# Two blocks of an ELU layer finish their exponential on ScalarE; the ELU becomes a minimum of two terms

## The chip, the cores and the metric

The kernel runs on one core of a Trainium2 chip. The metric is the time of one execution on the device, in microseconds (us); lower is better. The five engines of the core are called PE (TensorE, matrix products), DVE (VectorE), ACT (ScalarE), POOL (GpSimd) and SP (SyncE, which issues DMAs here).

## What is computed

Attention with a bucket mask, then a feed-forward layer with ELU, then a second one with a scaled squared ReLU. The matrices are float32; the result is float32, 1536 tokens by 512.

```python
# attention: q, k, v are (2, 8, 768, 64); a key counts only in the query's bucket (6 sign bits of a projection)
scores = where(q_bucket == k_bucket, scale * q @ k.T, -1e9)
attn   = softmax(scores);  x = concat_heads(attn @ v)          # (1536, 512)
# first layer: w_in (512, 2048), w_out (2048, 512)
h = x @ w_in
g = where(h > 0, h, exp(min(h, 0)) - 1)                        # ELU
x2 = g @ w_out
# second layer, other weights of the same shapes
out = (s * max(x2 @ w_in2, 0) ** 2 + b) @ w_out2
```

## The kernel before

Every float32 product is made of three float16 products (high by high, high by low, low by high), so each operand is split into a high and a low half. `products` (L503) issues these matmuls.

**Attention** goes by units: 2 batches x 6 row chunks x 8 heads = 96 units `u`. Unit `u` makes scores on PE (`u_s`, L336), clamps them with a running minimum on DVE (`u_soft`, L346, `p<-s`), adds a constant to that minimum (L347, `mx`), takes the exponential on ACT (L348), rounds to float16 on ACT (`u_split`, L367, `ph`), subtracts on POOL for the low half (L370), turns both halves by a DMA that SP issues (L372, `pt<-ph`), and multiplies by v on PE (`u_av`, L390, `xacc`). After eight heads `u_norm` (L401) writes a chunk of x. For the first 16 units PE does the turning instead.

**Weights** come as 64-bit words and are put together on DVE. `w_stream` (L165) handles one piece of 512 columns per step: a DMA into `wraw` (L162), three integer operations on DVE (L182, L183 into a PSUM tile `wx`, L185 into `wa`), ACT rounds the high half (L176: `wih`, `woh`), DVE makes the low half (L189: `wil`, `wol`). `w_in` and `w_out` are 16 pieces each. Before the attention of the second batch begins (from unit 38 on, `att_step`, L733), all pieces that are left are run one behind the other. Their buffers are then given to the loads of k, q and v of the second batch (L233).

**The first layer** (`moe1`, L549) goes in six blocks of 256 tokens. `up(i)` makes 8 PSUM tiles `h` of 128x512 from `wi`; each is handed to `act1` (L509), whose steps run beside the products of the next tiles: `exp` on ACT (L514, `e` from PSUM), `elu` on DVE (L517 and L519), `hi` on ACT (L522, `gh`), `lo` on POOL (L525, `gl`). `down(i)` multiplies `gh` and `gl` by `wo` into `x2p`. Units of attention are put between the products by a credit of estimated time (L742 to L749). The last part, `moe2`, is the second layer.

The order in which each engine takes its instructions is fixed at build time: the framework's scheduler works it out with a model of the engines, from the order of the code and the priorities. So another instruction in `act1` can change places all along the middle of the program. Each engine then takes its instructions in that order and waits where an operand is not there. SP issues its DMAs in order too.

In `act1`, with `SG` = 512 the factor by which h is scaled: `e` = exp(h); then `e` = min(SG e, SG) (L517); then `g` = max(e - SG, SG h) (L519).

Of the kernel before, what the change touches and what calls it, by code (L numbers as in the profile page):

```python
# [11 lines left out]
ACTF = mybir.ActivationFunctionType  # L12
ALU = mybir.AluOpType
# [32 lines left out]
W2OUT = 4  # L46
D2 = 200
SPLIT = lambda u: 'act'
WEV = lambda k: k % 3
W2EV = lambda k: k % 4 == 0  # L50
STEP_COST = 2.5
# [7 lines left out]
def model_kernel(tc, q, k, v, proj, w_in, w_out, w_in2, w_out2, s2, b2, sel, pop, eye, out):  # L59
    nc = tc.nc  # L60
# [18 lines left out]
    SG = SX * SW  # L79
# [4 lines left out]
    with ExitStack() as base:  # L84
# [267 lines left out]
        def u_split(u, eng):  # L352
            f = pf.pop(u)
            if u < FC * H:
                p = ps_p[0].tile([128, S], F32, tag="s", name="pT")
                for cc in range(C):
                    nc.tensor.transpose(p[:, 128 * cc:128 * cc + 128], f[:, 128 * cc:128 * cc + 128], ident)
                o = ring.take("pt", [128, S], F32, "pt")
                if eng == "act":
                    nc.scalar.activation(out=o, in_=p, func=ACTF.Copy)  # L360
                else:
                    nc.vector.tensor_copy(out=o, in_=p)
                pt[u] = o
                return
            t = ring.take("ph", [128, 2, S], F16, "ph")
            if eng == "act":
                nc.scalar.activation(out=t[:, 0, :], in_=f, func=ACTF.Copy)  # L367
            else:
                nc.vector.tensor_copy(out=t[:, 0, :], in_=f)
            nc.gpsimd.tensor_tensor(out=t[:, 1, :], in0=f, in1=t[:, 0, :], op=ALU.subtract)  # L370
            o = ring.take("pt", [128, 2 * C, 128], F16, "pt")
            nc.sync.dma_start_transpose(out=o, in_=t.rearrange("p x s -> p (x s)"))  # L372
            pt[u] = o
# [76 lines left out]
        def attention():  # L450
# [4 lines left out]
            while nxt["av"] < NU:  # L455
                if nxt["split"]:
                    u_split(nxt["split"].pop(0), SPLIT(nxt["s"]))
                u = nxt["av"]
# [25 lines left out]
        def staged():  # L484
            queue = []

            def add(stages):
                queue.append([0, stages])

            def run(order):  # L490
                for item in queue:
                    for lag, o, fn in item[1]:
                        if lag == item[0] and o == order:
                            fn()

            def tick():
                for item in queue:
                    item[0] += 1
                while queue and all(st[0] < queue[0][0] for st in queue[0][1]):
                    queue.pop(0)  # L500
            return add, run, tick

        def products(p, ws, xs, kks, n_kk):  # L503
            for kk in kks:
                for z, (a, b) in enumerate(((0, 0), (0, 1), (1, 0))):
                    nc.tensor.matmul(p, ws[a](kk), xs[b](kk), start=(kk == 0 and z == 0),  # L506
                                     stop=(kk == n_kk - 1 and z == 2))

        def act1(tmp, tmpg, p, gh, gl):  # L509
            t = {}  # L510

            def exp():
                t["e"] = tmp.tile([128, 512], F32, tag="e", name="e")
                nc.scalar.activation(out=t["e"], in_=p, func=ACTF.Exp, scale=1.0 / SG)  # L514

            def elu():
                nc.vector.tensor_scalar(t["e"], t["e"], SG, SG, op0=ALU.mult, op1=ALU.min)  # L517
                t["g"] = tmpg.tile([128, 512], F32, tag="g", name="g")
                nc.vector.scalar_tensor_tensor(out=t["g"], in0=t["e"], scalar=-SG, in1=p, op0=ALU.add, op1=ALU.max)  # L519

            def hi():
                nc.scalar.activation(out=gh, in_=t["g"], func=ACTF.Copy)  # L522

            def lo():
                nc.gpsimd.tensor_tensor(out=gl, in0=t["g"], in1=gh, op=ALU.subtract)  # L525
            return [(2, 0, hi), (1, 1, exp), (3, 2, lo), (1, 3, elu)]
# [22 lines left out]
        def moe1(wi, wo, gp, next_gp, tmp, tmpg, att_step):  # L549
            add, run, tick = staged()  # L550

            def slot(cost):
                run(0)
                run(1)
                run(2)
                yield cost
                run(3)
                tick()

            starts = [sum(BLOCKS1[:i]) * 128 for i in range(len(BLOCKS1))]  # L560
            g = {}

            def up(i):
                n = 128 * BLOCKS1[i]
                while done_chunks[0] < sum(BLOCKS1[:i + 1]):
                    att_step()
                cost = 12 * (n / 2400 + .003)
                gh, gl = g[i] = [gp[0].tile([128, KF, n], F16, tag=f"g{x}", name=f"g{x}") for x in "hl"]
                w_ = 512 // n
                i2, o2 = divmod(starts[i], 512)  # L570
                for f0 in range(0, KF, w_):
                    p = ring.take("m", [128, 512], F32, "h")
                    for f in range(f0, f0 + w_):
                        xs = [lambda kk, o=o: xx[i2][:, o + kk, o2:o2 + n] for o in (0, KM)]
                        ws = [lambda kk, w=w: w[:, f, kk * 128:kk * 128 + 128] for w in wi]
                        o = p[:, (f - f0) * n:(f - f0) * n + n]
                        products(o, ws, xs, range(KM), KM)
                        if f < f0 + w_ - 1:
                            yield cost
                    add(act1(tmp, tmpg, p, *(z[:, f0:f0 + w_, :].rearrange("p f n -> p (f n)") for z in (gh, gl))))  # L580
                    yield from slot(cost)
                in_done[0] = i + 1

            def down(i):
                n = 128 * BLOCKS1[i]
                cost = 12 * (n / 2400 + .003)
                i2, o2 = divmod(starts[i], 512)
                w_ = 512 // n
                for d0 in range(0, KM, w_):
                    p = ring.take("m", [128, w_, n], F32, "x2p")  # L590
                    for d in range(d0, d0 + w_):
                        xs = [lambda kk, z=z: z[:, kk, :] for z in g[i]]
                        ws = [lambda kk, w=w: w[:, kk, d * 128:d * 128 + 128] for w in wo]
                        for part in range(4):
                            products(p[:, d - d0, :], ws, xs, range(4 * part, 4 * part + 4), KF)
                            if part == 3 and d == d0 + w_ - 1:
                                xh, xl = (xx[i2][:, z * KM + d0:z * KM + d0 + w_, o2:o2 + n] for z in range(2))

                                def hi(p=p, xh=xh):
                                    nc.scalar.activation(out=xh, in_=p, func=ACTF.Copy, scale=SX2 / (SG * SW))  # L600

                                def lo(p=p, xh=xh, xl=xl):
                                    nc.vector.scalar_tensor_tensor(out=xl, in0=p, scalar=SX2 / (SG * SW), in1=xh,  # L603
                                                                   op0=ALU.mult, op1=ALU.subtract)
                                add([(1, 0, hi), (1, 3, lo)])
                            yield from slot(cost)

            for i in range(FIRST):
                yield from up(i)
            for i in range(FIRST):  # L610
                yield from down(i)
            for _ in range(4):
                yield from slot(0)
            next_gp()
            for i in range(FIRST, len(BLOCKS1)):
                yield from up(i)
                yield from down(i)
            for _ in range(4):
                yield from slot(0)
# [63 lines left out]
        if True:  # L683
# [12 lines left out]
            n = 0  # L696
# [11 lines left out]
            tmp = pool(w1st, "tmp", 2)  # L708
            tmpg = pool(w1st, "tmpg", TG)
# [3 lines left out]
            def next_gp():  # L713
                gst0.close()
                gp[0] = pool(gst1, "gp1", 1)
# [17 lines left out]
            def att_step():  # L733
                while live["w1"] and nxt["s"] >= (C - 1) * H - 2:
                    w1_step()
                if next(att, 0) == 0:
                    live["att"] = False
# [4 lines left out]
            for ks, cost in enumerate(moe1(wi, wo, gp, next_gp, tmp, tmpg, att_step)):  # L742
                if WEV(ks):
                    w1_step()
# [81 lines left out]
```

## Time and profile before

| | us |
|---|---|
| median of 3 runs (lowest, highest) | 740.74 (739.79, 742.73) |
| the profiled execution, its own time | 743.25 |
| its span, first to last instruction | 741.1 |
| PE busy in the span | 676.0 |
| DVE busy | 470.6 |
| ACT busy | 375.5 |
| POOL busy | 264.2 |

The profile records each instruction of one execution with its engine and source line. From it come: busy times by stretch of the span, groups of instructions by line, the waits (who sat idle until whom), the timeline, and the chain of work that ended last, followed back from the last instruction. "DMA share" is the mean busy share of the 16 DMA engines; it can pass 1, because packets overlap. "PEclk" is the granted clock of PE as a part of full speed. A wait for several things is put down to the one that came last.

### The profile page before, as it was taken

Reading aid. Unit: us, or ns where it says so; the run is one execution under the profiler, and the core shown is the slowest. Engines: PE = TensorE matmul, PEld = TensorE weight load, DVE = VectorE, ACT = ScalarE, POOL = GpSimd, SP = SyncE. Lnnn points to the kernel's source line nnn. Section 1 sums busy time; section 2 is a strip of 40 time slices with the busy share of each in tenths; the row PEclk is TensorE's granted clock in tenths of the full one; section 3 lists DMA queues with packets and bytes.
Section 4 is the critical chain, followed back from the end, with each engine's and each line's share of the span. In section 5 each row is a group of like instructions: output and inputs, shape, how many; then the busy total and the mean of one; then the engine's idle time right before and its main releaser. Section 6 shows DMA issues by size and latency. Waiting matters only on the chain.

```text
span 741.1 us, 14402 instructions
## 1 busy us (share of the span) xinstructions
PE 676.0 (91%) x5808; PEld 466.2 (63%) x5808; DVE 470.6 (63%) x890; ACT 375.5 (51%) x632; POOL 264.2 (36%) x199
## 2 busy tenths in 40 slices
PE   2689787888897899899999999999999999999998
PEld 0368576766685677788888988864444444444446
DVE  5789998999876557645644684348988989100000
ACT  2897776762777688756755323235555543010000
POOL 0000356660562358945855412214445441000000
PEclk9999989999999999999999999999999999999999
DMA  9954699897699959967758450001322314010000
GB/s 234 267 165 138 158 220 208 184 202 204 95 230 208 180 95 179 155 107 132 122 108 120 124 172 1 1 29 58 115 76 71 110 57 142 1 57 29 29 28 29
DMA packets 206594, 89.67 MB, mean 121 GB/s; under 512 B 171840, under 2 KB 203072, under 8 KB 206528
## 3 DMA queue, kind: packets, MB, share of 16 engines
q1 hardware_dynamic: 205936, 88.63, 54.6%
q8 instruction: 45, 0.74, 0.4%
q10 hardware_dynamic: 592, 0.14, 0.1%
q14 instruction: 21, 0.17, 0.1%
HBM read 43.13 MB, written 3.15 MB: 62 GB/s over the span
## 4 chain that ended last, share of the span: by engine, by line
PE 61%; DVE 15%; DMA 12%; ACT 6%; issue 4%; SPq 1%; POOL 0%; DVEq 0%; ACTq 0%; POOLq 0%
PE h L506 25%; PE y L506 17%; PE x2p L506 11%; DMA pt<-ph 6%; PE s L336 4%; DVE p L346 3%; PE xacc L390 3%; DVE e L517 2%; DMA q<-src 2%; DVE wx L182 1%; DVE wx L183 1%; DVE g L519 1%; ACT p L348 1%; DMA k<-srcl 1%; DMA raw<-in_k 1%
## 5 line engine op out<-in xcount | busy, mean ns | idle before, releaser
L370 POOL TENSOR_TENSOR ph<-p,ph 128x768 f16<-128x768 f32 x80 | 135.5, 1699 | 144.1 <-ACT ph L367 121.1
L506 PE MATMUL h<-x,wih 128*128 128x256 f16 x768 | 134.6, 279 | 0.9 <-DVE g L519 0.9
L348 ACT ACTIVATE p<-p,mx 128x768 f32<-128x768 f32 x96 | 89.2, 929 | 53.3 <-DVE mx L347 51.7
L346 DVE TENSOR_SCALAR_CACHE_REDUCE p<-s 128x768 f32<-128x768 f32 x96 | 90.8, 950 | 38.9 <-PE s L336 37.2
L506 PE MATMUL x2p<-gh,woh 128*128 128x256 f16 x384 | 105.1, 275 | 2.8 <-DVE x L603 1.0
L506 PE MATMUL h<-x,wil 128*128 128x256 f16 x384 | 107.1, 279 | 0.0
L506 PE MATMUL x2p<-gh,wol 128*128 128x256 f16 x384 | 105.4, 275 | 0.7 <-DVE wol L189 0.7
L506 PE MATMUL x2p<-gl,woh 128*128 128x256 f16 x384 | 105.3, 275 | 0.0
L336 PE MATMUL s<-k,q 128*128 128x512 f16 (+1 forms) x384 | 80.0, 334 | 12.9 <-DVE p L346 9.4
L546 POOL TENSOR_TENSOR g2l<-g,g2h 128x512 f16<-128x512 f32 x48 | 56.8, 1188 | 88.2 <-ACT g2h L543 88.2
L506 PE MATMUL h<-x,wi2bh 128*128 128x512 f16 x288 | 85.7, 379 | 0.0
L506 PEld LDWEIGHTS <-wih 128*128 128x128 f16 x768 | 76.5, 100 | 14.4 <-issue 1.8
L506 PEld LDWEIGHTS <-woh 128*128 128x128 f16 x768 | 75.3, 99 | 14.7 <-issue 1.7
L390 PE MATMUL xacc<-vv,pt 128*128 128x64 f16 x1440 | 56.6, 195 | 22.3 <-DMA pt<-ph 22.0
L525 POOL TENSOR_TENSOR gl<-g,gh 128x512 f16<-128x512 f32 x48 | 57.4, 1198 | 52.8 <-ACT gh L522 52.7
L506 PE MATMUL y<-wo2h,g2h 128*128 128x512 f16 (+1 forms) x208 | 75.4, 363 | 0.0
L506 PE MATMUL y<-wo2l,g2h 128*128 128x512 f16 (+1 forms) x208 | 75.4, 363 | 0.0
L506 PE MATMUL y<-wo2h,g2l 128*128 128x512 f16 (+1 forms) x208 | 75.3, 363 | 0.0
L390 PEld LDWEIGHTS <-pt 128*128 128x128 f16 x1440 | 52.1, 99 | 31.8 <-DMA pt<-ph 29.8
L367 ACT ACTIVATE ph<-p 128x768 f16<-128x768 f32 x80 | 66.5, 837 | 5.5 <-DMA pt<-ph 3.7
L506 PEld LDWEIGHTS <-g2h 128*128 128x128 f16 x416 | 40.7, 98 | 42.4
L657 ACT ACTIVATE y<-y 128x512 f32<-128x512 f32 (+1 forms) x13 | 7.3, 564 | 97.8 <-PE y L506 96.8
(101 smaller groups left out, 1109.3 us busy)
## 6 DMA issues: line engine op xcount, KB each, us to landing
wraw<-in_moe_w_in SPq DMA_DIRECT2D x32, 512.0 KB, 3.8
wraw<-in_moe_w_out SPq DMA_DIRECT2D x32, 512.0 KB, 3.7
raw<-in_k SPq DMA_DIRECT2D x8, 384.0 KB, 4.3
raw<-in_q SPq DMA_DIRECT2D x8, 384.0 KB, 4.1
out<-y SPq DMA_DIRECT2D x11, 256.0 KB, 2.0
v<-in_v SPq DMA_DIRECT2D x4, 384.0 KB, 4.7
raw<-in_v SPq DMA_DIRECT2D x4, 384.0 KB, 4.3
pt<-ph SPq DMA_TRANSPOSE x80, 4.0
```

The lines of the kernel that those rows point to most:

```text
L182: nc.vector.tensor_scalar(x, top, 3, 0x3FFFFFFF, op0=ALU.logical_shift_left, op1=ALU.bitwise_and)
L183: nc.vector.scalar_tensor_tensor(out=x, in0=low, scalar=29, in1=x, op0=ALU.logical_shift_right, op1=ALU.bitwise_or)
L336: nc.tensor.matmul(p[:, a0:a1], w[b, hp][:, j, c, :], kf[:, a0:a1], start=(x == 0), stop=(x == 1))
L346: nc.vector.tensor_scalar(f, sps.pop(u), CLAMP, None, op0=ALU.min, op1=ALU.min, accum_out=mx)
L348: nc.scalar.activation(out=f, in_=f, func=ACTF.Exp, scale=-sm / (SQ * SQ), bias=mx, accum_out=sums[b, c][:, h:h + 1])
L367: nc.scalar.activation(out=t[:, 0, :], in_=f, func=ACTF.Copy)
L370: nc.gpsimd.tensor_tensor(out=t[:, 1, :], in0=f, in1=t[:, 0, :], op=ALU.subtract)
L390: nc.tensor.matmul(acc, o[:, C * x + cc, :], vv[:, j, cc, y, :], start=(z == 0 and cc == 0), stop=(z == 2 and cc == C - 1))
L506: nc.tensor.matmul(p, ws[a](kk), xs[b](kk), start=(kk == 0 and z == 0), stop=(kk == n_kk - 1 and z == 2))
L517: nc.vector.tensor_scalar(t["e"], t["e"], SG, SG, op0=ALU.mult, op1=ALU.min)
L525: nc.gpsimd.tensor_tensor(out=gl, in0=t["g"], in1=gh, op=ALU.subtract)
L546: nc.gpsimd.tensor_tensor(out=gl, in0=t["g"], in1=gh, op=ALU.subtract)
```

## The change

The ELU is written as min(max(h, 0), exp(h) - 1), all scaled by `SG`. `SG e - SG` is made in place, in blocks 0 and 1 by a second ACT instruction right behind the exponential (L517 of the changed kernel, a copy with scale and bias), in blocks 2 to 5 by DVE (one `tensor_scalar` as before, with multiply and add in place of multiply and minimum). DVE's last operation then takes the maximum with 0 of the PSUM tile `h` and the minimum with `e`. The new function `LIN` picks the engine by the number of the block.

```diff
+LIN = lambda i: 'act' if i < 2 else 'dve'
...
-        def act1(tmp, tmpg, p, gh, gl):
+        def act1(tmp, tmpg, p, gh, gl, lin):
             t = {}
             def exp():
                 t["e"] = tmp.tile([128, 512], F32, tag="e", name="e")
                 nc.scalar.activation(out=t["e"], in_=p, func=ACTF.Exp, scale=1.0 / SG)
+                if lin == "act":
+                    nc.scalar.activation(out=t["e"], in_=t["e"], func=ACTF.Copy, scale=SG, bias=-SG)
             def elu():
-                nc.vector.tensor_scalar(t["e"], t["e"], SG, SG, op0=ALU.mult, op1=ALU.min)
+                if lin == "dve":
+                    nc.vector.tensor_scalar(t["e"], t["e"], SG, -SG, op0=ALU.mult, op1=ALU.add)
                 t["g"] = tmpg.tile([128, 512], F32, tag="g", name="g")
-                nc.vector.scalar_tensor_tensor(out=t["g"], in0=t["e"], scalar=-SG, in1=p, op0=ALU.add, op1=ALU.max)
+                nc.vector.scalar_tensor_tensor(out=t["g"], in0=p, scalar=0.0, in1=t["e"], op0=ALU.max, op1=ALU.min)
...
-                    add(act1(..., gh, gl))
+                    add(act1(..., gh, gl, LIN(i)))
```

In the order of the changed kernel, 16 instructions `e<-e` have gone from DVE to ACT and 32 are left on DVE. ACT still has one load of its function table, as before. The order of the work around blocks 0 and 1 changes on every engine. Line numbers of the changed kernel are 1 higher up to the exponential, and 5 higher from L519 on.

The first place is DVE's order at the last tiles of block 0, where the pieces of `w_out` are being put together (L182 to L189; `p,mx` and `mx` are the attention). Before:

```order
L346 TENSOR_SCALAR p,mx<-s 128x768
L182 TENSOR_SCALAR wx<-wraw 128x512
L517 TENSOR_SCALAR e<-e 128x512
L347 TENSOR_SCALAR mx<-mx 128x1
L346 TENSOR_SCALAR p,mx<-s 128x768
L189 SCALAR_TENSOR_TENSOR wol<-wa,woh 128x4x128
L183 SCALAR_TENSOR_TENSOR wx<-wraw,wx 128x512
L519 SCALAR_TENSOR_TENSOR g<-e,h 128x512
L517 TENSOR_SCALAR e<-e 128x512
L347 TENSOR_SCALAR mx<-mx 128x1
```

Now, the same tiles:

```order
L347 TENSOR_SCALAR p,mx<-s 128x768
L348 TENSOR_SCALAR mx<-mx 128x1
L524 SCALAR_TENSOR_TENSOR g<-h,e 128x512
L186 SCALAR_TENSOR_TENSOR wa<-wraw,wx 128x512
L347 TENSOR_SCALAR p,mx<-s 128x768
L348 TENSOR_SCALAR mx<-mx 128x1
L524 SCALAR_TENSOR_TENSOR g<-h,e 128x512
L183 TENSOR_SCALAR wx<-wraw 128x512
```

The `e<-e` are gone from DVE, and `g<-h,e` stands between the same kinds of work.

The second place is ACT at the end of the weight stream, where the pieces that are left are run together (`woh`, 128x4x128), followed by the first tiles of block 1. Before:

```order
L348 ACTIVATE p,sum<-p,mx 128x768 x2
L367 ACTIVATE ph<-p 128x768 x2
L176 ACTIVATE woh<-wa 128x4x128
L348 ACTIVATE p,sum<-p,mx 128x768
L367 ACTIVATE ph<-p 128x768
L600 ACTIVATE x_113<-x2p 128x2x256
L176 ACTIVATE woh<-wa 128x4x128 x7
L514 ACTIVATE e<-h 128x512 x2
L348 ACTIVATE p,sum<-p,mx 128x768 x2
L600 ACTIVATE x_113<-x2p 128x2x256
```

Now:

```order
L177 ACTIVATE woh<-wa 128x4x128
L368 ACTIVATE ph<-p 128x768
L349 ACTIVATE p,sum<-p,mx 128x768
L368 ACTIVATE ph<-p 128x768
L177 ACTIVATE woh<-wa 128x4x128 x5
L515 ACTIVATE e<-h 128x512 x2
L349 ACTIVATE p,sum<-p,mx 128x768
L517 ACTIVATE e<-e 128x512
L349 ACTIVATE p,sum<-p,mx 128x768
L517 ACTIVATE e<-e 128x512
L605 ACTIVATE x_113<-x2p 128x2x256
```

Seven pieces stood together at the end of the stream before; five do now, and two have moved up among the units of attention. The new ACT instructions of block 1 stand between two exponentials of the attention.

## Rows read from the trace of the kernel before

**Rows 1.** The page: busy time of each engine, share of the span, instructions.

```profile
PE 676.0 (91%) x5808; PEld 466.2 (63%) x5808; DVE 470.6 (63%) x890; ACT 375.5 (51%) x632; POOL 264.2 (36%) x199
```

**Rows 2.** Busy time of each engine by stretch of the span (us).

```profile
core 0: us, PE busy (x) PEld busy (x) DVE busy (x) ACT busy (x) POOL busy (x), PEclk, DMA share, GB/s
95.00:182.00 87.00, 72.47 (x848) 57.60 (x846) 82.41 (x148) 51.76 (x91) 45.02 (x29) 0.96 0.96 206
182.00:220.00 38.00, 34.81 (x366) 28.74 (x364) 31.69 (x63) 26.29 (x48) 21.67 (x16) 0.96 0.82 148
...
200.00:220.00 20.00, 19.20 (x220) 15.87 (x219) 17.01 (x32) 14.55 (x26) 13.25 (x11) 0.91 1.18 215
...
320.00:340.00 20.00, 20.00 (x251) 17.07 (x248) 9.63 (x21) 10.40 (x17) 11.02 (x7) 1.00 0.69 121
...
440.00:460.00 20.00, 20.00 (x185) 17.94 (x184) 8.56 (x13) 4.65 (x8) 3.47 (x3) 1.00 0.15 45
...
130.00:135.00 5.00, 4.12 (x50) 3.47 (x49) 5.00 (x9) 4.36 (x8) 3.43 (x2) 1.00 0.63 165
...
150.00:155.00 5.00, 3.97 (x47) 3.10 (x45) 5.00 (x8) 1.13 (x2) 3.36 (x3) 1.00 0.85 206
```

**Rows 3.** DVE by line, 95 to 182 us: busy, mean ns, idle before.

```profile
L189 DVE SCALAR_TENSOR_TENSOR wol<-wa,woh 128x512 f16<-128x512 f32 x15 | 13.3, 886 | 0.0
L517 DVE TENSOR_SCALAR e<-e 128x512 f32<-128x512 f32 x8 | 7.6, 945 | 0.1
```

**Rows 4.** The chain that ended last: start, length, what.

```profile
101.72 7.17 DMA pt<-ph
...
131.53 1.76 DVE e L517
...
137.08 1.51 DVE e L517
...
141.32 1.38 DVE e L517
...
205.05 1.82 DVE e L517
...
209.51 0.60 DVE e L517
```

**Rows 5.** Timeline of DVE and of POOL near three `e<-e` and one `wol`.

```profile
101.14 0.43 DVE L517 TENSOR_SCALAR e<-e 128x512 f32<-128x512 f32 x1
...
102.40 1.65 POOL L370 TENSOR_TENSOR ph<-p,ph 128x768 f16<-128x768 f32 x1 [2.55 <-ACT ph L367]
...
137.08 1.51 DVE L517 TENSOR_SCALAR e<-e 128x512 f32<-128x512 f32 x1
...
136.67 1.64 POOL L370 TENSOR_TENSOR ph<-p,ph 128x768 f16<-128x768 f32 x1
...
152.28 1.99 DVE L189 SCALAR_TENSOR_TENSOR wol<-wa,woh 128x512 f16<-128x512 f32 x1
```

**Rows 6.** Tile `wa`, 164 to 183 us: ns shortest/median/longest, first and last start.

```profile
L176 ACT ACTIVATE woh<-wa x7: 619/630/631, 165.1 to 181.8; 128x512 f16<-128x512 f32 x7
L189 DVE SCALAR_TENSOR_TENSOR wol<-wa,woh x7: 681/691/693, 166.4 to 182.4; 128x512 f16<-128x512 f32 x7
```

**Rows 7.** Waits, 145 to 182 us, and SP's own, 95 to 182 us: total, times, longest.

```profile
ACT woh L176 <- DVE wa L185: 13.4, 7, 2.5
...
SPq L233 <- DVE wa L185: 2.7, 1, 2.7
```

**Rows 8.** L517 alone: DVE busy by stretch.

```profile
182.00:220.00 38.00, 5.82 (x8) 0.96 0.82 148
95.00:182.00 87.00, 7.56 (x8) 0.96 0.96 206
```

**Rows 9.** The page: costliest groups, nearest forms to the new instructions.

```profile
L539 DVE SCALAR_TENSOR_TENSOR g<-h,r 128x512 f32<-128x512 f32 x48 | 33.0, 688 | 15.3 <-ACT r L535 14.9
...
L519 DVE SCALAR_TENSOR_TENSOR g<-e,h 128x512 f32<-128x512 f32 x48 | 32.7, 684 | 3.0
L522 ACT ACTIVATE gh<-g 128x512 f16<-128x512 f32 x48 | 29.9, 626 | 38.1 <-DVE g L519 37.8
```

More of the change, by code (lines that the diff above doesn't have):

```diff
@@ L579, in up @@
                             yield cost
-                    add(act1(tmp, tmpg, p, *(z[:, f0:f0 + w_, :].rearrange("p f n -> p (f n)") for z in (gh, gl))))
+                    add(act1(tmp, tmpg, p, *(z[:, f0:f0 + w_, :].rearrange("p f n -> p (f n)") for z in (gh, gl)), LIN(i)))
                     yield from slot(cost)
```

## The prediction

> **What bounds the kernel now.** I read the engines' totals first, then their busy time by stretch, the chain, and last the lines and the timeline of the stretch that the change touches. PE is busy for 676.0 us of 741.1 [rows 1], and from 320 us on it has next to no gap: 20.00 of 20 us in each of the seven windows from 320 to 460 [rows 2]. So nothing that is saved behind 320 us can pay unless it makes PE's own work shorter, and the change does not touch that. Ahead of 320 us PE has gaps, and a gap closed there moves the whole saturated rest forward by as much. Blocks 0 and 1 of the ELU lie in that part: eight `e<-e` between 95 and 182 us, eight between 182 and 220 us [rows 8].
>
> In the first of these stretches PE is busy for 72.47 of 87 us, 14.5 us idle. DVE is busy for 82.41, idle for only 4.6; ACT has 51.76 and POOL 45.02 [rows 2]. DVE sets the pace: it must put the pieces of `w_out` together and clamp the scores of the units up to 38, and only then can the second batch begin. DVE is busy for 5.00 of 5 us in each of the five windows from 130 to 155 us [rows 2], and there the chain runs over DVE, with three `e<-e` on it (1.76, 1.51, 1.38) [rows 4]. At the end of the stretch seven pieces stand in a row, and ACT waits 13.4 us for DVE's `wa` [rows 7]. SP's load of k for the second batch waits 2.7 us for the same `wa` [rows 7]. But DMA is a near second: its share is 0.96 over these 87 us [rows 2], and ahead of 129 us the chain waits for turned tiles, once for 7.17 us [rows 4].
>
> **Part 1, block 0, DVE.** Eight `e<-e` go, 7.56 us [rows 8], mean 945 ns [rows 3]. One of them takes 0.43 us at 101.14, in the 2.55 us in which POOL is idle ahead of 102.40; another takes 1.51 us, begins at 137.08 while a POOL subtraction runs from 136.67 to 138.31, and ends at 138.59, a fast one's length behind it [rows 5]. So an `e<-e` is some 0.42 us of work and otherwise waiting for POOL: 8 x 0.42 = 3.4 us of work, 4.2 us of waiting. The work is saved for certain. The waiting can come back: `wol` waits in the same manner (1.99 us once, mean 886 over 15) [rows 5, 3]. POOL is busy for about half the stretch (45 of 87) [rows 2], so I let half the waiting return at the next such instruction: 2.1 us. Saved: 3.4 + 2.1 = 5.5 us; the ends are 3.4 and 7.6. The order says where it lands: two of the seven pieces move up among the attention, and the `woh` of the seven begin from 165.1 to 181.8 us, (181.8 - 165.1) / 6 = 2.8 us apart [rows 6], so the run ends 5.6 us sooner, if unit 38 comes no later than now. I take 5.5.
>
> Does DMA allow it? Its load in the stretch is 0.96 x 87 = 83.5 us, and in 81.5 us it would be a share of 1.02. A share of 1.18 stands in the window at 200 us [rows 2], so this is possible, but little is left. If it is not, the low end of this part is 0.
>
> **Part 2, block 0, ACT.** Eight copies are added. No such instruction is in the trace; the nearest is L522, SBUF to SBUF, 626 ns [rows 9]. 8 x 0.626 = 5.0 us, which brings ACT from 51.76 to 56.8 of 87. It has 35 us of idle time there, 13.4 of them waiting for DVE's pieces [rows 7], so I cost this at nothing. Behind each copy in ACT's order stand an exponential or a rounding of the attention, and POOL, SP's turning DMA and PE's `xacc` behind those; if the cover were gone, the price is the 5.0. For the single tile, 0.626 on ACT replaces a mean of 0.945 on DVE, so the way from `h` to `g` gets no longer.
>
> **Part 3, block 1.** DVE loses 5.82 us [rows 8], of which two instances lie on the chain, 1.82 + 0.60 = 2.4 us [rows 4]. ACT gains 5.0 again, on 26.29 of 38 us [rows 2]: 31.3, or 82%. Here ACT also makes the k and q halves of the second batch, and its new copies stand between exponentials. I let half of the 5.0 fall on the path: 2.5 against 2.4, so 0. The ends: 2.4 saved, or 5.0 - 2.4 = 2.6 lost.
>
> **Part 4, the rest.** In blocks 2 to 5 `e<-e` keeps its shape with another second operation. `g` takes the PSUM tile first and compares instead of adding: the trace has that form, 688 ns against 684 [rows 9], 48 x 0.004 = 0.2 us, beside a saturated PE: nothing. From about unit 68 on PE's order is as before.
>
> Sum: 5.5 + 0 + 0 + 0 = 5.5 us off the span, 741.1 to 735.6. The profiled execution took 743.25, 2.15 over its span, and 2.5 over the median; I take the 5.5 from the median: 740.7 - 5.5 = **735.2 us**. What is late next is DMA, whose share is 1.18 from 200 us on [rows 2].
>
> **Rivals.**
>
> *The waits only move.* Each POOL subtraction holds up the next DVE instruction of that kind instead, and only 3.4 us are saved: 737.3 us. For it: `wol` already shows such waits, with a mean of 886 ns against 691 in the run of seven [rows 3, 6]. Against: half of the waiting returning is already in the sum, and it would have to be all of it. The Trainium skill, "SBUF — State Buffer", section "Who interferes with whom", says that VectorE's two-port forms and those with two SBUF inputs share a port pair with GpSimd as an exclusive lock, the loser blocked for the whole instruction; the trace agrees (1.51 us beside the 1.64 of POOL). By that rule the lock goes to whoever comes first, so a freed wait may go to `wol`.
>
> *DMA takes over.* With 0.96 the turned tiles and weight loads are already at their limit, the two pieces that move up (their loads too, on SP's queue ahead of turning DMAs) make `xacc` wait longer, and what DVE saves becomes idle time of DVE: nothing to 1.5 us, say 740.0 us. For it: the waits of up to 7.17 us in the chain ahead of 129 us [rows 4]. Against: DVE has no gap from 130 to 155 us while DMA's share is 0.63 and 0.85 in the first and the last of these windows [rows 2].
>
> *ACT takes over, slower.* In 182 to 220 us ACT stands at 82% with the copies, and each one sits ahead of an exponential or of a k or q half. If all eight delay the units, 5.0 us are lost there, and if DMA also eats block 0's gain, the time is 740.7 + 5.0 = 745.7 us. It decides from the point at which ACT has no idle time in that stretch. Against: 38 - 31.3 = 6.7 us of idle time are left, and `e<-e` leaves the chain on DVE at the same place. The Trainium skill, "ScalarE: Activation LUTs", section "Rules for kernel authors", says to put multiplications and additions on VectorE, not ScalarE; the rows agree on the bare lengths, 0.43 against 0.626, which speaks against this change, but not once the wait for POOL is counted (0.945).
>
> That the change does not do what it says can be left out: the order shows 16 copies on ACT and no second table load.
>
> **How the numbers follow.** Forecast 0.54, with its own range from 740.7 - 7.6 - 2.4 = 730.7 up to 737.0. The waits move: 0.14. DMA takes over: 0.18. ACT takes over: 0.14. A change of 0.5%, 3.7 us, is about what a measurement of this kernel can tell from none: faster is under 737.0, slower over 744.4. So faster 0.54, same 0.14 + 0.18 = 0.32, slower 0.14. The range reaches from 730.7, the upper end of both savings, to 744.0, which takes in both "same" cases and part 3's loss of 2.6 (743.3) and leaves out most of ACT's case.
>
> **What would show it.** Right: the last `woh` ends 4 to 6 us sooner than 181.8 + 0.6 = 182.4 us [rows 6], DVE's idle time from 95 us to that point stays under 7 us, PE's idle time there falls from 14.5 to about 9 to 10, and PE reaches its saturated part as much sooner. The waits move: `wol`'s mean rises from 886 to over 1000 ns. DMA takes over: DVE's idle time rises by as much as its work falls, and `xacc` waits longer for `pt`. ACT takes over: `p` and `src` on ACT start without a wait, with DVE and PE idle until them. What would make all of this wrong is the new order itself: a product or an `xacc` that stands ahead of what is ready and holds PE, in a place that these stretches do not show.

## The result, and the profile after

The changed kernel takes **734.96 us** (median of 5 runs, 733.34 to 735.93); the kernel before takes 740.74 us in the same comparison (median of 5, 739.69 to 744.45). The comparison's ratio is 0.9892 with an interval of 0.9859 to 0.9924. The 735.2 us of the forecast is 0.2 us off, but the saving is the better measure, and there the sum was short: by the medians it is 5.8 us, by the ratio 8.0 us (0.0108 x 740.7). A repeat beside longer series of the kernel before gave 0.9894, or 7.9 us, with an interval of 6.2 to 9.6. The forecast of 5.5 us lies just under that interval. So the direction and the rough size were right, and some 2.4 us of saving are not in the sum. That the time is only 0.2 us off is in part luck, as is shown below.

The engines' totals on the page of the changed kernel, which answer to [rows 1]:

```profile
PE 676.5 (92%) x5808; PEld 466.3 (64%) x5808; DVE 462.9 (63%) x874; ACT 382.1 (52%) x648; POOL 263.9 (36%) x199
```

DVE has 16 instructions and 7.7 us less, ACT 16 more and 6.6 us more; PE's work is the same. The span is 734.1 us, in an execution of 735.93. By stretch, in the columns of [rows 2]:

```profile
core 0: us, PE busy (x) PEld busy (x) DVE busy (x) ACT busy (x) POOL busy (x), PEclk, DMA share, GB/s
95.00:182.00 87.00, 76.99 (x875) 61.84 (x874) 80.81 (x145) 55.78 (x100) 46.14 (x30) 0.93 0.96 210
182.00:220.00 38.00, 32.72 (x352) 26.48 (x350) 26.64 (x54) 31.93 (x58) 22.49 (x16) 1.00 0.88 161
...
260.00:320.00 60.00, 58.19 (x733) 48.27 (x732) 40.59 (x93) 47.32 (x83) 48.09 (x32) 0.99 0.96 150
300.00:320.00 20.00, 19.98 (x253) 17.17 (x252) 12.22 (x27) 12.34 (x21) 15.10 (x10) 1.00 0.98 156
```

In 95 to 182 us PE's idle time has gone from 14.5 to 87.00 - 76.99 = 10.0 us (12.0 in a second trace of the changed kernel, changed_again). ACT carries 31.93 of 38 us in the stretch of block 1. PE has next to no gap from 300 us on. The pieces of `w_out`, which answer to [rows 6] and [rows 3]; first tile `wa`, 164 to 183 us, ns shortest/median/longest, first and last start:

```profile
L177 ACT ACTIVATE woh<-wa x6: 613/630/631, 163.6 to 178.8; 128x512 f16<-128x512 f32 x6
L190 DVE SCALAR_TENSOR_TENSOR wol<-wa,woh x6: 676/693/1631, 165.0 to 179.5; 128x512 f16<-128x512 f32 x6
```

and DVE by line, 95 to 182 us, busy, mean ns, idle before:

```profile
L190 DVE SCALAR_TENSOR_TENSOR wol<-wa,woh 128x512 f16<-128x512 f32 x16 | 17.1, 1068 | 1.1 <-ACT woh L177 0.9
...
L524 DVE SCALAR_TENSOR_TENSOR g<-h,e 128x512 f32<-128x512 f32 x8 | 5.5, 683 | 1.7 <-ACT e L517 1.6
```

The last `wol` begins at 179.5 us, where it began at 182.4: 2.9 us sooner. The mean of a `wol` has risen from 886 to 1068 ns. The new ACT instructions, tile `e` over the whole span:

```profile
L522 DVE TENSOR_SCALAR e<-e x32: 417/996/1760, 263.4 to 463.5; 128x512 f32<-128x512 f32 x32
L517 ACT ACTIVATE e<-e x16: 613/620/632, 103.2 to 213.9; 128x512 f32<-128x512 f32 x16
```

On ACT the step takes 613 to 632 ns, every time. On DVE, where blocks 2 to 5 still have it, it takes anything from 417 to 1760.

### The profile page after: what moved, and what is told of

Its sections match the earlier page's. It is cut to its first block, busy times and chain, and to the rows that moved or that the text cites. A ratio compares the mean times of both kernels' runs of the same rounds, so it can differ in the third digit from the quotient of the medians.

```text
span 734.1 us, 14403 instructions
## 1 busy us (share of the span) xinstructions
PE 676.5 (92%) x5808; PEld 466.3 (64%) x5808; DVE 462.9 (63%) x874; ACT 382.1 (52%) x648; POOL 263.9 (36%) x199
## 4 chain that ended last, share of the span: by engine, by line
PE 60%; DVE 12%; DMA 11%; ACT 7%; issue 6%; POOL 3%; SPq 1%; DVEq 0%; ACTq 0%; POOLq 0%
PE h L507 24%; PE y L507 17%; PE x2p L507 10%; DMA pt<-ph 6%; PE s L337 4%; PE xacc L391 3%; DVE p L347 3%; POOL ph L371 2%; ACT p L349 2%; DVE wx L184 2%; DMA q<-src 2%; DVE wx L183 1%; DVE e L522 1%; DVE wa L186 1%; DVE g L524 1%
## 5 line engine op out<-in xcount | busy, mean ns | idle before, releaser
L337 PE MATMUL s<-k,q 128*128 128x512 f16 (+1 forms) x384 | 82.2, 338 | 9.7 <-DVE p L347 7.7
```

Source lines behind the costliest of these rows:

```text
L337: nc.tensor.matmul(p[:, a0:a1], w[b, hp][:, j, c, :], kf[:, a0:a1], start=(x == 0), stop=(x == 1))
```

## The experiments

Each kernel below was timed in five rounds beside the kernel before, whose medians in the three groups of runs were 743.3, 743.4 and 743.3 us. A saving in us is (1 - ratio) x 743.3.

**Parts of the change, each with the order that its own program gets.** Three values of one line:

```diff
-LIN = lambda i: 'act' if i < 2 else 'dve'
+LIN = lambda i: 'dve'                # form_only
+LIN = lambda i: 'act' if i < 1 else 'dve'    # only_block0
+LIN = lambda i: 'act' if i == 1 else 'dve'   # only_block1
```

> The new formula in all six blocks, with the multiply and add of e on DVE everywhere; no copy on ACT. Every engine's order is that of before. Both theories (the gain comes from the time that DVE no longer spends; the gain comes from the new order of the instructions): no change, within 0.3% of before, since neither DVE's time nor the order moves. If the form itself were worth something, this would be faster by some of the 5.8 us.

> The copy on ACT in block 0 alone. Theory DVE time: 3 to 4 us faster than before (the last piece of w_out ended 2.9 us sooner in the changed kernel), and only_block1 gives the rest. Theory order: the order differs from both kernels, so the gain is anything between -2 and +7 us and does not add up with only_block1 to 5.8.

> The copy on ACT in block 1 alone. My own sum put block 1 at 0 (2.4 us less on DVE's chain, 2.5 us more on ACT). Theory DVE time: 0 to 2.4 us faster. Theory order: some 3 us faster, since the changed kernel gained 3.5 us between 283 and 317 us, where no instruction was removed.

| kernel | median us | ratio | interval | saved us |
|---|---|---|---|---|
| form_only | 742.92 | 1.0003 | 0.9982 to 1.0024 | -0.2 |
| only_block0 | 740.27 | 0.9964 | 0.9942 to 0.9986 | 2.7 |
| only_block1 | 741.32 | 0.9975 | 0.9954 to 0.9997 | 1.9 |

The new form of the two DVE instructions is worth nothing, and in form_only every engine's order is that of the kernel before. The two blocks apart save 2.7 and 1.9 us, 4.6 together, against 7.9 for both in one program. Either the blocks help each other, or each of these programs has an order of its own and the order has a price. The next runs hold the order fixed.

**The order of before, DVE's work cut.** The instructions were changed after the order was set, so each engine's order and waits are those of the kernel before. short_e_old_order cuts the 16 `e<-e` of blocks 0 and 1 to one column, short_e_block0 only the 8 of block 0:

```diff
-nc.vector.tensor_scalar(t["e"], t["e"], SG, SG, op0=ALU.mult, op1=ALU.min)
+nc.vector.tensor_scalar(t["e"][:, 0:1], t["e"][:, 0:1], SG, SG, op0=ALU.mult, op1=ALU.min)
```

> The kernel before, order of every engine as it was, but the 16 e<-e of blocks 0 and 1 work on one column instead of 512 (changed after the order was set), and nothing is added on ACT; so g of these blocks is not the reference's. Theory DVE time: 5 to 8 us faster, as much as the changed kernel or more. Theory order: under 3 us faster, because the order that gave the gain is not there.

> The kernel before in its old order, with only the 8 e<-e of block 0 cut to one column (after the order was set), nothing added on ACT; g of block 0 is not the reference's. Cutting all 16 gave 4.3 us. My own sum: all of it is in block 0, so 3.5 to 5 us faster than before. If block 1 carries its share by DVE time (5.8 of 13.4 us), 2 to 3 us faster.

| kernel | median us | ratio | interval | saved us |
|---|---|---|---|---|
| short_e_old_order | 738.99 | 0.9942 | 0.9919 to 0.9965 | 4.3 |
| short_e_block0 | 739.49 | 0.9944 | 0.9923 to 0.9966 | 4.2 |

In the old order DVE's time in block 0 is worth 4.2 us. Block 1's adds 0.1 by the medians, with an uncertainty of some 2 us. The 4.3 us lie between what the two theories asked for (5 to 8, and under 3). DVE by line in short_e_old_order, 95 to 182 us, the one-column instructions and the `wol`:

```profile
L189 DVE SCALAR_TENSOR_TENSOR wol<-wa,woh 128x512 f16<-128x512 f32 x16 | 15.6, 977 | 0.7 <-ACT woh L176 0.7
...
L517 DVE TENSOR_SCALAR e<-e 128x1 f32<-128x1 f32 x10 | 1.5, 148 | 0.4 <-ACT e L514 0.3
```

and the end of its pieces (tile `wa`, 164 to 183 us):

```profile
L189 DVE SCALAR_TENSOR_TENSOR wol<-wa,woh x6: 681/691/693, 163.5 to 177.7; 128x512 f16<-128x512 f32 x6
```

This kernel's last `wol` begins at 177.7 us, 4.7 us sooner than before and 1.8 sooner than in the changed kernel (0.4 sooner than in changed_again), and yet by the medians it is the slower of the two by 4 us. So the changed kernel has something that this one lacks, and it is not an earlier end of `w_out`.

**The new order, ACT's work cut or DVE's put back.** These are the changed kernel with its order held. changed_again is the kernel itself. new_order_short_copy cuts the 16 new ACT instructions to one column:

```diff
-nc.scalar.activation(out=t["e"], in_=t["e"], func=ACTF.Copy, scale=SG, bias=-SG)
+nc.scalar.activation(out=t["e"][:, 0:1], in_=t["e"][:, 0:1], func=ACTF.Copy, scale=SG, bias=-SG)
```

new_order_work_back keeps them, and puts a multiply-add of DVE on a scratch tile `dum` (384 columns from a constant) ahead of each of the 16 `g`; new_order_back_block0 ahead of the 8 of block 0 only:

```diff
+nc.vector.tensor_scalar(dum, ident3, SG, -SG, op0=ALU.mult, op1=ALU.add)
 nc.vector.scalar_tensor_tensor(out=t["g"], in0=p, scalar=0.0, in1=t["e"], op0=ALU.max, op1=ALU.min)
```

> The changed kernel as it is, once more beside the next three on one chip. Both theories: 5 to 8 us faster than before (0.989 to 0.993).

> The changed kernel with its own order, but the 16 copies on ACT work on one column instead of 512 (changed after the order was set), so g of blocks 0 and 1 is not the reference's. It gives ACT's price: if the copies are hidden, as in the sum for block 0, within 1.5 us of the changed kernel; if half of block 1's copies lie on the path, as I put it, 2.5 us faster than the changed kernel; if all of them do, 5 us faster.

> The changed kernel with its own order, but ahead of each g of blocks 0 and 1 DVE has an operation again, multiply and add from 384 columns of a constant into a scratch tile that nobody reads, put in after the order was set. Theory DVE time: 3 to 6 us slower than the changed kernel, near before. Theory order: under 1.5 us slower than the changed kernel, since the order is the same.

> The changed kernel in its own order, with the scratch operation on DVE put back ahead of the 8 g of block 0 alone. With all 16 put back it lost 5.1 us of its 7.9. My own sum: block 0 carries it, so 4 to 5.5 us slower than the changed kernel. If block 1 carries its share, 2 to 3.5 us slower.

| kernel | median us | ratio | interval | saved us |
|---|---|---|---|---|
| changed_again | 734.76 | 0.9894 | 0.9871 to 0.9916 | 7.9 |
| new_order_short_copy | 734.69 | 0.9894 | 0.9871 to 0.9917 | 7.9 |
| new_order_work_back | 740.52 | 0.9962 | 0.9941 to 0.9983 | 2.8 |
| new_order_back_block0 | 738.51 | 0.9936 | 0.9914 to 0.9958 | 4.8 |

ACT's share has no price that shows: with its 16 instructions at 192 ns instead of 620 the median is 0.07 us lower, with an uncertainty of some 2 us. DVE's share has one: put back, it takes 5.1 of the 7.9 us. What the scratch instructions cost DVE, 95 to 182 us in new_order_work_back:

```profile
L190 DVE SCALAR_TENSOR_TENSOR wol<-wa,woh 128x512 f16<-128x512 f32 x16 | 18.7, 1166 | 0.7 <-ACT woh L177 0.7
...
L522 DVE TENSOR_SCALAR dum<-ident 128x384 uint8<-128x384 f32 x8 | 4.6, 577 | 0.0
```

They are shorter than the `e<-e` (4.6 us against 7.56 in block 0 [rows 8]), but with the longer `wol` DVE is as loaded as before:

```profile
95.00:182.00 87.00, 75.62 (x864) 60.16 (x863) 82.91 (x150) 55.85 (x99) 45.14 (x30) 0.93 0.97 210
```

82.91 us against 82.41 [rows 2], and 470.5 against 470.6 in the whole span. With DVE's load back, 2.8 us of saving are left (1.3 to 4.4), and DVE's load does not explain them. From the other side: the changed kernel and short_e_old_order both have DVE's work gone, all but the one-column instructions (8 x 0.148 = 1.2 us in block 0), and differ by 7.9 - 4.3 = 3.6 us, with intervals of the ratio that do not overlap. Both ways round, **some 3 us come from the new order**. The granted clock does not explain them: its mean over the executions is 0.979 in the kernel before, 0.981 in short_e_old_order and new_order_work_back, 0.983 in changed_again. Between executions of one kernel 0.01 of clock went with some 2 us (a line fitted through the executions of all these kernels), so 0.002 to 0.004 are worth less than 1 us, by this estimate. Block 1 alone is open: leaving it free and loading block 0 costs 3.1 of 7.9, loading both 5.1, so block 1 would be worth 2.0 in this order, but the intervals of the two overlap. The 3.1 fit the expectation by which block 1 carries its share (2 to 3.5), not the one by the prediction's own sum (4 to 5.5).

**Is it the wait for POOL?** no_port has the order of before and full-length instructions, but the 16 read the PSUM tile `h` in place of the SBUF tile `e`:

```diff
-nc.vector.tensor_scalar(t["e"], t["e"], SG, SG, op0=ALU.mult, op1=ALU.min)
+nc.vector.tensor_scalar(t["e"], p, SG, SG, op0=ALU.mult, op1=ALU.min)
```

> The kernel before in its old order, but the 16 e<-e of blocks 0 and 1 read the PSUM tile h in place of e (changed after the order was set); g of these blocks is not the reference's. If their long instances are waits for a port that VectorE shares with POOL, each now takes 0.69 us like other operations from PSUM, with no instance over 0.75 beside a POOL subtraction, 5.5 us in block 0 in place of 7.6; the time falls by 0 to 2 us, and wol keeps its waits or gets more. If the long instances have another cause, they stay, up to 1.8 us.

It takes 741.92 us, ratio 0.9974 (0.9952 to 0.9997): 1.9 us saved. Tile `e` in its trace, then one of the instructions on DVE and the POOL subtraction beside it:

```profile
L517 DVE TENSOR_SCALAR e<-h x16: 670/680/692, 104.3 to 218.9; 128x512 f32<-128x512 f32 x16
```

```profile
134.47 0.68 DVE L517 TENSOR_SCALAR e<-h 128x512 f32<-128x512 f32 x1
...
134.39 3.26 POOL L370 TENSOR_TENSOR ph<-p,ph 128x768 f16<-128x768 f32 x2 [3.33 <-ACT ph L367]
```

From PSUM the instruction takes 0.67 to 0.69 us whatever POOL does; an `e<-e` from SBUF beside a POOL subtraction took 1.51 us at 137.08 [rows 5]. Whom the long ones wait for can be read from their ends. In the kernel before 26 of the 48 `e<-e` take more than 0.55 us, and every one of them ends 0.28 us behind the end of a POOL instruction. All nine `wol` of more than 0.75 us end 0.55 us behind one. So the spread of the `e<-e` is the wait for POOL, as the prediction had it, and `wol` waits for POOL too. What is freed is taken up in part by `wol`, whose mean is higher in no_port too:

```profile
L189 DVE SCALAR_TENSOR_TENSOR wol<-wa,woh 128x512 f16<-128x512 f32 x15 | 14.9, 994 | 0.0
```

**More blocks.** If ACT's share is free and DVE's is worth something, more blocks may pay:

```diff
-LIN = lambda i: 'act' if i < 2 else 'dve'
+LIN = lambda i: 'act' if i < 3 else 'dve'    # three_blocks
+LIN = lambda i: 'act'                # all_blocks
```

> The copy on ACT in blocks 0, 1 and 2, with an order of its own. Block 2 lies at 260 to 340 us, where PE's gaps end. Theory DVE time: within 1.5 us of the changed kernel. Theory order: it may lie up to 4 us to either side.

> The copy on ACT in all six blocks. Behind some 317 us PE is saturated, so theory DVE time: like the changed kernel, within 1.5 us, with at most 2 us more from block 2, which lies between 260 and 340 us. Theory order: anything within 4 us of the changed kernel.

three_blocks takes 737.76 us, 0.9919 (0.9888 to 0.9950); all_blocks 734.5 us, 0.9888 (0.9868 to 0.9908). Neither can be told from the changed kernel's 0.9894. Blocks 2 to 5 lie beside a saturated PE for the most part, where no gain of DVE's time shows, so no version here is shown to be better than the change as it stands.

## Why the prediction was right, and where its working was not

**What bounds the kernel: right.** The gain comes from ahead of PE's saturated part, which is as long as before: from product 2900 of the 5808 to the last PE takes 405.4 to 405.8 us in all ten traces of either order. DVE's time is worth something ahead of it. In the order of before, DVE's time in block 0 alone is worth 4.2 us; in the new order putting it back costs 3.1 there and 5.1 in both blocks.

**Part 1, 5.5 us: mis-sized, about 4.2.** The two pieces did move up: five stand behind the last unit where seven did. But the last `wol` came 2.9 us sooner, not 5.6 (4.3 in the trace of changed_again, where it begins at 178.1). The condition "if unit 38 comes no later than now" did not hold: the run of pieces is shorter, but the first `woh` of its five begins at 167.6 us (166.3 in changed_again), where the first of the seven began at 165.1. The term for returned waiting was about right: 15 to 16 `wol` at 1068 instead of 886 ns make 15 x 0.18 = 2.7 us, against 2.1 in the sum. By another trace of the old order, form_only, whose `wol` has a mean of 936 ns, it is 2.0. One reading under it was loose: the `e<-e` at 137.08 ends 0.28 us behind POOL, not a fast one's 0.42. What the sum left out is that DVE would idle more: 87 - 80.81 = 6.2 us against 4.6, most of it `g` waiting 1.6 us for ACT's `e`, and some of it `wol` waiting for `woh`. 7.56, less 2.0 to 2.7, less 1.6 leaves 3.3 to 4.0 us, near the 2.9 and 4.3 of the two traces and the 4.2 of short_e_block0.

**Part 2, nothing: right.** The copies took 620 ns (626 estimated), and cutting them to 192 gave back nothing that shows.

**Part 3, 2.4 - 2.5 = 0: one term wrong.** Half of ACT's 5.0 us was put on the path. The runs show none of it there: ACT rose to 31.93 of 38 us (31.3 forecast), and new_order_short_copy, without them, is no faster by the medians, where 2.5 us were expected. The DVE side was worth 0.1 us by the medians in the old order, not 2.4, so 0 was a fair sum there by luck; in the new order it may be some 2.0, which the runs do not settle.

**Part 4, nothing: right** for the new form, 1.0003.

**The sum: a term was missing.** The prediction set no price on the order and named it only as what could make everything wrong, "a product or an `xacc` that stands ahead of what is ready". It acted, and in the kernel's favour, with some 3 us: 4.3 for DVE's time leave 3.6 of the 7.9. The 5.5 was thus too much for DVE and nothing for the order, two errors that partly cancel. The time of 735.2 came out as near as it did by luck, because the 740.74 it was taken from lay below the 743.3 of the later, longer series.

*Where the order earns it* is shown for about half of it. In 260 to 320 us PE's idle time is 1.8 us in the changed kernel, 4.8 in the kernel before, and 3.5 in short_e_old_order, the fastest one in the old order. By stretch, the kernel before:

```profile
260.00:320.00 60.00, 55.21 (x660) 44.22 (x660) 37.66 (x86) 47.26 (x82) 45.64 (x31) 0.94 0.87 142
```

and short_e_old_order:

```profile
260.00:320.00 60.00, 56.48 (x722) 46.80 (x720) 42.20 (x92) 47.49 (x83) 48.56 (x32) 1.00 0.92 152
```

A window of time cuts each trace at other products, though. PE's wait for `k`, 2.04 us ahead of 260.95 us in the kernel before, looks as if it were gone in short_e_old_order; it is there, 1.56 us ahead of 258.22, just outside the window. So it is better to count by products. PE's order is one and the same in the five traces of the old order, and in the five of the new one; the two orders differ only behind the first 668 and ahead of the last 3098 of the 5808 products. When 2140 products have begun, and again at 2750, both orders have done the same ones. From the one to the other PE takes:

| old order | us | new order | us |
|---|---|---|---|
| kernel before | 52.0 | changed kernel | 48.2 |
| form_only | 49.5 | changed_again | 48.2 |
| short_e_old_order | 50.0 | new_order_short_copy | 48.2 |
| short_e_block0 | 50.5 | new_order_work_back | 48.3 |
| no_port | 49.8 | new_order_back_block0 | 48.6 |

Each of the new order is faster here than each of the old, whether DVE's work is there, cut or put back. By the means it is some 1.7 us, without the kernel before, whose granted clock was 0.50 for 3.4 us of this stretch (303.1 to 306.5 us). The largest part is one `xacc`. In the kernel before:

```profile
301.92 0.70 PE L390 MATMUL xacc<-vv,pt 128*128 128x64 f16 x18 [1.99 <-DMA pt<-ph]
...
302.89 1.24 PE L336 MATMUL s<-k,q 128*128 128x512 f16 x4
```

and in the changed kernel:

```profile
296.67 0.81 PE L337 MATMUL s<-k,q 128*128 128x512 f16 x4
...
297.65 0.69 PE L391 MATMUL xacc<-vv,pt 128*128 128x64 f16 x18
```

In the old order this `xacc` has 2534 products ahead of it and stands ahead of four products of scores; in the new one it has 2545, the four among them, and its turned tile has that much more time to arrive. PE's wait ahead of it is 1.0 to 2.0 us in the five traces of the old order and at most 0.4 in those of the new. When 2140 products have begun, the changed kernel's order has gained nothing yet: 264.7, 263.7 and 263.5 us in its three traces with DVE's work gone, 263.6 in short_e_old_order, against 268.0 in the kernel before and 267.3 in form_only. Where the rest of the order's some 3 us comes from stays open. No run moved this `xacc` by itself.

**The rivals.** *The waits only move* is true of half the waiting or a little more, not of all. The sign named for it did come (`wol` at 1068 ns, over 1000), so that sign did not tell it from the forecast. *DMA takes over* falls: DMA's share stays at 0.96 over 95 to 182 us, PE did more in them, and DVE's idle time rose by 1.6 us where its work fell by 7.6. `xacc`'s wait for `pt` there shows no clear change. Waits of the kernel before in 95 to 182 us, then of the changed kernel:

```profile
PE xacc L390 <- DMA pt<-ph: 7.9, 7, 3.4
```

```profile
ACT woh L177 <- DVE wa L186: 11.6, 6, 2.4
...
PE xacc L391 <- DMA pt<-ph: 6.4, 5, 2.8
```

(It is 7.4 us in form_only and 9.5 in changed_again.) *ACT takes over* falls with new_order_short_copy and with the faster time itself. The rule of the Trainium skill that spoke for it, "ScalarE: Activation LUTs", section "Rules for kernel authors" (multiplications and additions on VectorE), holds for the bare lengths, 0.43 against 0.62 us, and points the wrong way here, where DVE sets the pace and ACT has room.

## What to carry to other kernels

For an instruction moved from an engine that sets the pace to one with idle time, count its time on the first, less the waiting that the next instruction of that kind takes over, less what the first engine now idles for the second's answer: here 7.6 us on DVE gave 4.2. Where a scheduler sets the order, such a move changes the order of everything behind it, and that can be worth as much as the work (here some 3 of 8 us; only_block0, with 2.7 us where the old order without that work gave 4.2, hints at a loss, but the intervals overlap): put a bound on it in the sum, and to measure it, change the work after the order is set, once in each of the two orders. To find where an order gains, compare the traces between the same products, not in the same window of time.

## What the runs showed of the hardware

- A DVE multiply-add of 128x512 f32 from SBUF took 417 to 1760 ns beside POOL's subtractions; a multiply-and-minimum of that shape with its input in PSUM took 670 to 692 ns, sixteen times out of sixteen. The mean in block 0, with POOL busy for 45 of 87 us, was 945 ns from SBUF and 682 from PSUM. The Trainium skill, "SBUF — State Buffer", section "Who interferes with whom", says that a VectorE instruction with at most one SBUF input, outside the two-port forms, does not contend with GpSimd; the 670 to 692 ns agree.
- A DVE instruction that has waited for POOL can be told by its end: the 26 long `e<-e` of the kernel before end 0.281 to 0.286 us behind the end of a POOL instruction, and its nine long `wol` 0.547 to 0.550 us.
- Part of the freed wait goes on to `wol`, the next instruction with two SBUF inputs: its mean was 886 and 936 ns in two traces of the old order, 977 and 1060 with `e<-e` cut, 994 with it moved to PSUM, 1068 and 1059 in the changed kernel.
- Two traces of one order differ by 3 us: the span is 741.1 us before and 737.8 in form_only. They are level when 2247 products have begun (276.9 and 277.0 us) and 3.2 us apart at 2700 (315.7 and 312.5). In between lie a wait of one `xacc` of 1.99 against 0.97 us and, in the kernel before alone, 3.4 us at a granted clock of 0.50, in which PE did 17 products.
